# Attention with a threshold, followed by a two-layer MLP: q and k loads moved to SyncE's DMA queue, weights used two steps later

## The chip, the cores and the metric

The kernel runs on one core of a Trainium2 chip. Its engines run side by side, each with an instruction stream of its own: TensorE (PE), VectorE (DVE), ScalarE (ACT), GpSimd (POOL) and SyncE (SP), which here only issues DMAs and waits. All DMAs of the core share 16 DMA engines, whichever engine issues them. The metric is the device time of one execution in microseconds. Lower is better.

## What is computed

```python
scores = q @ k.T / sqrt(64)                       # 8 batches x 8 heads, 576 rows, 64 dims
thresh = max(scores, axis=-1) - tau               # tau = 0.02
scores = where(scores >= thresh, scores, -1e9)
attn   = softmax(scores)
x      = (attn @ v), heads side by side           # [4608, 512]
h      = x @ w_in                                 # [512, 2048]
out    = maximum(0.01 * h, h) @ w_out             # [2048, 512], result [4608, 512] fp32
```

## The kernel before

**Steps.** The attention is cut into 144 steps, 18 per batch. A step takes 128 rows of one pair of heads: its scores go to PSUM on PE (lines 333 and 339), DVE scales them and finds the row maxima (two instructions of line 393, one per head), ACT and POOL add the threshold (518, 519), DVE cuts off below it (548), and one step later ACT takes the exponential of each head (553). q and k are held as two fp16 parts (high and low), so each score is a sum of three products.

**Units and turns.** Two steps form a unit (one step in parts of the last batch). Two steps after a unit's last step, SP issues a DMA that transposes the unit's attention weights from tile w to tile wt (line 542; this is called a turn). The turn of a full unit moves 20 blocks of 128x128 fp16. A unit's last step has an odd number in its batch, so these turns are issued at odd steps. `LAG` steps after the unit's last step, PE multiplies v by the turned weights (pv, line 364), and DVE scales the result into xT, the input of the MLP (lines 374 and 380; the scale comes from wt too). From step `ENDS` = 130 on, units use `LAGE` = 4 in place of LAG. There are four wt buffers (`NWT`) and four w buffers (`NW`), two v buffers and one PSUM buffer for pv.

**The MLP.** When all four head pairs of a row block are in xT, its h units (8 matmuls each, line 248 through the helper of line 238) are put in a queue, and behind them its o units (4 matmuls each, line 265). A step takes at most one of each from the queues. ACT and DVE apply the leaky ReLU (252, 218), DVE copies a finished block of 128 output rows to osb (274), and SP stores it at the start of the next step (275). After the last step the rest of the queues is run without scores (lines 565 to 578).

**Order of the work around the change.** The order is written out by hand: the loop of line 491 puts each step's instructions in place, and two lists (`tick`, `ptick`) give what else is issued at the end of which step. The constants give the steps, counted from the start of the batch before the one that is loaded:

```python
LOADS = ((-6, 0), (2, 4))      # k and q of the first half, k and q of the second half
TURNS = ((8, 10), (14, 16))    # turns of split k and q, the same halves
VS = (-6, 0, 2, 4)             # four pieces of v, counted from the batch's own start
WOUTS = (0, 2, 4, 6, 8, 10, 12, 14)
```

`load_half` (line 95) loads k of two head pairs with one DMA (line 102) and q with two (line 105), 576 KB in each case, into tiles km and qm with two buffers each. ACT (line 156) and POOL (160, 166) split them into tiles ks and qs, and SP turns these (line 178) to kst and qst. The first batch is loaded before the loop, split by ACT and DVE, and turned by PE (line 189). v comes through POOL's queue with a cast to fp16 (line 128), as do w_in (410) and w_out (415); in the first batch these wait for an instruction of that step. So SP's queue holds, in order within a step: stores of the step before, the turn of a unit's weights, then turns of q or k. ACT's queue holds the loads of q and k between its activations.

Of the kernel before, what the change touches and what calls it, by code (L numbers as in the profile page):

```python
# [16 lines left out]
def kernel(  # L17
# [22 lines left out]
    nc = tc.nc  # L40
# [3 lines left out]
    DM = moe_w_in.shape[0]  # L44
    DF = moe_w_in.shape[1]
    C = 1.0 / (64.0 * 64.0 * 8.0)
    LAG = 5
    NARROW = 0
    NJ = DF // 128
    NEG = -1025.0  # L50
# [23 lines left out]
    if tau_f > 1.0:  # L74
# [10 lines left out]
        out=ident, in_=ident, compare_op=AX.is_equal, fill=0.0, base=0, pattern=[[-1, 128]], channel_multiplier=1)  # L85
# [9 lines left out]
    def load_half(src, store, nm, b, hb):  # L95

        m = store[b, hb] = sb.tile([128, 2, 576], FP32, tag=nm, bufs=2, name=nm)
        in_ = src[b, :, :, :].rearrange("(h f) (p t) d -> f p h (t d)", h=2, t=9)[ds(2 * hb, 2)]  # L100
        if nm == "km":
            nc.scalar.dma_start(out=m, in_=in_.rearrange("f p h x -> (f p) h x"))
        else:
            for f in range(2):
                nc.scalar.dma_start(out=m.rearrange("(p f) h x -> f p h x", f=2)[f], in_=in_[f])

    anchor = [None]

# [101 lines left out]
    def next_h():  # L210
        return hq.popleft()[0] if hq else None

    def next_o():
        return oq.popleft()[0] if oq else None
# [189 lines left out]
    for hb in range(2):  # L404
        load_half(k, kms, "km", 0, hb)
        load_half(q, qms, "qm", 0, hb)
# [50 lines left out]
    for b in range(1, B):  # L457
        s0 = 18 * (b - 1)
        for hb in range(2):
            t0 = s0 + (PREP1 if b < 2 else PREP)[hb]  # L460
            at(s0 + LOADS[hb][0], lambda b=b, hb=hb: load_half(k, kms, "km", b, hb))
            at(s0 + LOADS[hb][1], lambda b=b, hb=hb: load_half(q, qms, "qm", b, hb))
            at(t0 - 1, lambda b=b, hb=hb: hi("k", b, hb))
            at(t0 + 1, lambda b=b, hb=hb: hi("q", b, hb))

            for i, what in enumerate(("k0x", "k0l", "k1x q0x", "k1l", "q0l", "q1x", "q1l")):
                for w in what.split():
                    nm, h = w[0], int(w[1])
                    if w[2] == "x":
                        at(t0 + i, lambda nm=nm, h=h, b=b, hb=hb: after_anchor(x64(nm, b, hb, h)), ptick)  # L470
                    else:
                        for part in PARTS[nm]:
                            at(t0 + i, lambda nm=nm, h=h, b=b, hb=hb, part=part: after_anchor(lo(nm, b, hb, h, part)), ptick)
            at(s0 + TURNS[hb][0], lambda b=b, hb=hb: turn("k", b, hb))
            at(s0 + TURNS[hb][1], lambda b=b, hb=hb: turn("q", b, hb))
        for i in range(4):
            at(18 * b + VS[i], lambda b=b, i=i: load_v(b, i))
# [4 lines left out]
    for ui in range(len(units)):  # L482
        last = units[ui][3] + size[ui] - 1
        lag = LAGN if units[ui][0] < NARROW else LAG if last < ENDS else LAGE
        pv_at.setdefault(last + lag, []).append(ui)
# [4 lines left out]
    done = None  # L490
    for s in range(NS + LAG + 1):
        live = s < NS
# [6 lines left out]
        while credit >= 1.0:  # L499
            f = next_o()  # L500
            if f:
                ou.append(f)
            f = next_h()
# [8 lines left out]
        if live:  # L512
# [7 lines left out]
                out=P_[:, 0, :], in0=sa, scalar1=1.0, scalar2=bb[:, 0:1], op0=AX.mult, op1=AX.add)  # L520
            prev = (P_,) + unit_of[s]
        leak()
        for i in range(max(len(ou), len(hu))):
            o = ou[i]() if i < len(ou) else None
            h = hu[i]() if i < len(hu) else None
# [7 lines left out]
        if now is not None:  # L533
# [5 lines left out]
                out=W_[:, :, 1152:1280].rearrange("p i (h r) -> p i h r", h=2),  # L539
# [3 lines left out]
                out=uwt[now][:, 0:nw].rearrange("p i j r -> p (i j) r"), in_=W_.rearrange("p i c -> p (i c)"),  # L543
                transpose=True)
        if last is not None:
# [6 lines left out]
            for h in range(2):  # L552
                nc.scalar.activation(  # L553
                    out=uW[ui][:, i, ds(576 * h, 576)], in_=P_[:, h, :], func=AF.Exp, bias=exp_bias, scale=1.0,
# [14 lines left out]
    while hq or oq or leaky:  # L569
        for nx in (next_o, next_h):  # L570
            leak()
            f = nx()
            if f:
                f = f()
# [39 lines left out]
```

## Time and profile before

| what | value |
|---|---|
| time, median of 3 runs | 559.02 us (557.1, 559.02, 574.88) |
| the profiled execution: its time | 557.1 us |
| its span (first to last instruction) | 555.4 us |
| mean granted clock of TensorE | 0.945 |
| ACT, POOL busy | 76%, 50% of the span |
| moved by DMA | 101.79 MB, mean 183 GB/s |
| SP's DMA queue (q1), POOL's (q0), ACT's (q10) | 77.1%, 12.2%, 11.1% of 16 engines' span |
| loads of k (line 102), median issue to landing | 6.4 us, 16 of 576 KB |
| loads of q (line 105) | 5.4 us, 32 of 288 KB |
| pieces of v (line 128) | 5.4 and 6.1 us, 32 |
| turns of weights (line 542) | 6.5 us, 76 |
| stores (line 275) | 3.2 us, 36 of 256 KB |

In the views, "A <- B" means that A's engine stood idle until B was done; a DMA counts from its issue to its landing. The row of DMA digits cuts the span into 40 slices, 9 meaning 90% or more. A line of the timeline gives the start, the length, the engine (SPq and ACTq are the queues that issue DMAs), the line of the kernel and the tiles. The length of an issue on SP is the time that SP needs until it can issue the next one.

### The profile page before, as it was taken

Reading aid. Unit: us, or ns where it says so; the run is one execution under the profiler, and the core shown is the slowest. Engines: PE = TensorE matmul, PEld = TensorE weight load, DVE = VectorE, ACT = ScalarE, POOL = GpSimd, SP = SyncE. Lnnn points to the kernel's source line nnn. Section 1 sums busy time; section 2 is a strip of 40 time slices with the busy share of each in tenths; the row PEclk is TensorE's granted clock in tenths of the full one; section 3 lists DMA queues with packets and bytes.
Section 4 is the critical chain, followed back from the end, with each engine's and each line's share of the span. In section 5 each row is a group of like instructions: output and inputs, shape, how many; then the busy total and the mean of one; then the engine's idle time right before and its main releaser. Section 6 shows DMA issues by size and latency. Waiting matters only on the chain.

```text
span 555.4 us, 13438 instructions
## 1 busy us (share of the span) xinstructions
PE 473.1 (85%) x4912; PEld 294.6 (53%) x4912; DVE 464.1 (84%) x1213; ACT 424.3 (76%) x924; POOL 278.6 (50%) x476
## 2 busy tenths in 40 slices
PE   4637648898948989899888989998969999999996
PEld 3414325554625656555555655565635665666673
DVE  4936739998948999899988999999978999999641
ACT  5755728978748888888788988988886988888531
POOL 5246914668417664468446763667445764332000
PEclk9855669999979999999999999999998999999999
DMA  8999999989999899989999999989997999976611
GB/s 208 234 218 156 168 160 207 219 150 219 186 183 195 157 217 181 269 143 230 180 254 167 193 224 217 239 173 217 196 196 162 201 195 175 155 137 137 115 39 57
DMA packets 279426, 101.79 MB, mean 183 GB/s; under 512 B 254273, under 2 KB 266561, under 8 KB 279361
## 3 DMA queue, kind: packets, MB, share of 16 engines
q1 hardware_dynamic: 257344, 73.15, 77.1%
q0 software_dynamic: 13056, 8.92, 12.2%
q10 hardware_dynamic: 8960, 18.88, 11.1%
q8 instruction: 38, 0.62, 0.4%
q14 instruction: 28, 0.22, 0.1%
HBM read 36.70 MB, written 9.44 MB: 83 GB/s over the span
## 4 chain that ended last, share of the span: by engine, by line
DVE 29%; DMA 29%; issue 14%; PE 12%; POOL 11%; ACT 4%; ACTq 0%; POOLq 0%; SPq 0%; DVEq 0%
DMA wt<-w 23%; DVE sf L393 12%; DVE gT L218 5%; DVE P L548 5%; DMA v<-in_v_dram 5%; PE sc L333 4%; POOL P L519 4%; PE op L238 3%; DVE w L538 3%; PE pv L364 3%; POOL qs L166 2%; ACT w L553 2%; POOL ks L166 2%; PE hp L238 2%; DVE osb L274 2%
## 5 line engine op out<-in xcount | busy, mean ns | idle before, releaser
L393 DVE TENSOR_SCALAR_CACHE_REDUCE sf<-sc 128x576 f32<-128x576 f32 x288 | 205.4, 749 | 16.1 <-PE sc L333 15.8
L553 ACT ACTIVATE w<-P 128x576 f16<-128x576 f16 x288 | 193.8, 674 | 7.2 <-DVE P L548 2.3
L518 ACT ACTIVATE P<-sf,bb 128x576 f16<-128x576 f32 x144 | 111.3, 773 | 93.7 <-POOL bb L517 89.8
L238 PE MATMUL hp<-xT,win 128*128 128x256 f16 (+1 forms) x1344 | 151.9, 259 | 0.0
L238 PE MATMUL op<-wout,gT 128*128 128x512 f16 x576 | 148.8, 382 | 2.0 <-DVE osb L274 1.7
L333 PE MATMUL sc<-kst,qst 64*128 64x320 f16 (+1 forms) x1536 | 134.5, 301 | 11.7 <-DVE sf L393 11.2
L238 PEld LDWEIGHTS <-win 128*128 128x128 f16 x1344 | 117.7, 99 | 43.4 <-issue 2.3
L519 POOL TENSOR_SCALAR P<-sf,bb 128x576 f16<-128x576 f32 x139 | 106.0, 762 | 14.2 <-POOL bb L517 0.2
L364 PE MATMUL pv<-wt,v 128*64 128x256 f16 (+2 forms) x1000 | 59.8, 257 | 57.4 <-DMA wt<-w 52.0
L218 DVE SCALAR_TENSOR_TENSOR gT<-hp,gT 128x512 f16<-128x512 f32 x144 | 98.4, 683 | 11.3 <-ACT gT L252 11.3
L517 POOL TENSOR_SCALAR bb<-mx 128x2 f32<-128x2 f32 x139 | 27.9, 201 | 157.4 <-DVE sf L393 144.1
L333 PEld LDWEIGHTS <-qst 64*128 64x128 f16 x1536 | 73.3, 99 | 61.2 <-issue 41.2
L252 ACT ACTIVATE gT<-hp 128x512 f16<-128x512 f32 x144 | 83.5, 580 | 16.4 <-PE hp L238 16.4
L548 DVE TENSOR_SCALAR P<-P 128x1152 int16<-128x1152 int16 x144 | 81.4, 565 | 0.0
L364 PEld LDWEIGHTS <-v 128*64 128x64 f16 x1000 | 41.6, 114 | 74.5 <-issue 65.8
L238 PEld LDWEIGHTS <-gT 128*128 128x128 f16 x576 | 45.9, 98 | 64.1 <-issue 28.5
L374 DVE TENSOR_TENSOR xT<-pv,wt 128x128 f16<-128x128 f32 x128 | 32.0, 293 | 37.6 <-PE pv L364 37.5
L553 ACT ACTIVATION_READ_ACCUMULATOR w<-P 128x1 f32 x288 | 53.9, 187 | 0.0
L166 POOL TENSOR_TENSOR ks<-km,ks 128x320 f16<-128x320 f32 (+1 forms) x56 | 39.8, 731 | 9.2 <-DVE P L548 8.6
L166 POOL TENSOR_TENSOR qs<-qm,qs 128x576 f16<-128x576 f32 x28 | 35.8, 1278 | 12.4 <-DVE P L548 12.4
L538 DVE TENSOR_SCALAR w<-rc 128x256 f16<-128x256 f32 (+1 forms) x76 | 37.8, 497 | 2.6
L128 POOL DMA_DIRECT2D v<-in_v_dram x32 | 20.9, 653 | 16.9 <-DVE P L548 5.8
(35 smaller groups left out, 211.4 us busy)
## 6 DMA issues: line engine op xcount, KB each, us to landing
km<-in_k_dram ACTq DMA_DIRECT2D x16, 576.0 KB, 6.4
qm<-in_q_dram ACTq DMA_DIRECT2D x32, 288.0 KB, 5.4
out_dram<-osb SPq DMA_DIRECT2D x36, 256.0 KB, 3.2
v<-in_v_dram POOLq DMA_DIRECT2D x16, 160.0 KB, 6.1
v<-in_v_dram POOLq DMA_DIRECT2D x16, 128.0 KB, 5.4
win<-in_moe_w_in_dram POOLq DMA_DIRECT2D x8, 256.0 KB, 11.5
wout<-in_moe_w_out_dram POOLq DMA_DIRECT2D x8, 256.0 KB, 10.6
wt<-w SPq DMA_TRANSPOSE x76, 6.5
```

What stands on the lines that cost most here:

```text
L166: return nc.gpsimd.tensor_tensor(out=dst[:, h], in0=src[:, h], in1=h_[:, h], op=AX.subtract)
L218: nc.vector.scalar_tensor_tensor(out=G.g[u], in0=hp, scalar=0.01, in1=G.g[u], op0=AX.mult, op1=AX.add)
L238: nc.tensor.matmul(out=out_, lhsT=lhsT, rhs=rhs, start=start, stop=stop, skip_group_check=True)
L252: nc.scalar.activation(out=G.g[u], in_=hp, func=AF.Relu, bias=0.0, scale=0.99)
L333: nc.tensor.matmul(out=sc[h][:, cols], lhsT=qt[r, qi, ds(2 * c, 2)].rearrange("d t a b -> d (t a b)")[:, g::2], rhs=rhs, start=(i == 0), s ...
L364: nc.tensor.matmul(out=o_[ds(64 * h, 64)], lhsT=vt[:, pp, h, j, :], rhs=w_[:, :, 4 * h + j, :], start=(j == 0), stop=(j == 4), skip_group_ ...
L393: nc.vector.tensor_scalar(out=sf, in0=sc[h][:, ds(SC0, 576)], scalar1=C, scalar2=None, op0=AX.mult, op1=AX.max, accum_out=mx[:, h : h + 1])
L518: nc.scalar.activation(out=P_[:, 1, :], in_=sB, func=AF.Identity, bias=bb[:, 1:2], scale=1.0)
L519: (nc.vector if s < SPOOL else nc.gpsimd).tensor_scalar(out=P_[:, 0, :], in0=sa, scalar1=1.0, scalar2=bb[:, 0:1], op0=AX.mult, op1=AX.add)
L538: nc.vector.tensor_scalar(out=W_[:, :, 1152:1280].rearrange("p i (h r) -> p i h r", h=2), in0=rc[:, 0:nw, :].unsqueeze(3).to_broadcast([12 ...
L548: anchor[0] = nc.vector.tensor_scalar(out=pi, in0=pi, scalar1=NEG, scalar2=None, op0=AX.max)
L553: nc.scalar.activation(out=uW[ui][:, i, ds(576 * h, 576)], in_=P_[:, h, :], func=AF.Exp, bias=exp_bias, scale=1.0, accum_out=usm[ui][:, i, ...
```

## The change

LAG goes from 5 to 7, so pv of a unit stands seven steps after its last step (four from step 130 on, as before). The loads of q and k are issued by SP instead of ACT, at the same steps, behind SP's turn of the weights of the step before and behind the step's store. The first batch's loads move too. The loop runs for two steps more. The loads' sizes, the steps at which they and the turns stand, and the loads of v, w_in and w_out are the same.

```diff
-    LAG = 5
+    LAG = 7
...
         if nm == "km":
-            nc.scalar.dma_start(out=m, in_=in_.rearrange("f p h x -> (f p) h x"))
+            nc.sync.dma_start(out=m, in_=in_.rearrange("f p h x -> (f p) h x"))
         else:
             for f in range(2):
-                nc.scalar.dma_start(out=m.rearrange("(p f) h x -> f p h x", f=2)[f], in_=in_[f])
+                nc.sync.dma_start(out=m.rearrange("(p f) h x -> f p h x", f=2)[f], in_=in_[f])
```

## The prediction

> **What bounds the kernel now.** I read four views in this order. First the page's busy shares and slices:
>
> ```profile
> span 555.4 us, 13438 instructions
> ...
> PE 473.1 (85%) x4912; PEld 294.6 (53%) x4912; DVE 464.1 (84%) x1213; ACT 424.3 (76%) x924; POOL 278.6 (50%) x476
> ...
> DMA  8999999989999899989999999989997999976611
> ```
>
> No engine is full, two are close, and the DMA engines are busy in nearly every slice. Second, the waits: who stops PE and DVE?
>
> ```profile
> PE pv L364 <- DMA wt<-w: 52.0, 26, 10.0
> DVE xT L374 <- PE pv L364: 37.5, 19, 9.7
> PE pv L364 <- DMA v<-in_v_dram: 5.1, 5, 2.0
> ```
>
> (Total us, times, longest.) PE runs in program order, so when pv waits for its turned weights, everything stops. That is 57.1 us of PE standing still for two transfers; DVE idles behind it. Third, the chain of waits, start and length, where the transfer is shown from its issue to its landing, and the same place on SP's queue, on ACT's and on PE:
>
> ```profile
> 34.06 13.02 DMA wt<-w
> ...
> 61.37 15.21 DMA wt<-w
> ...
> 257.27 8.40 DMA wt<-w
> ...
> 521.06 3.63 DMA wt<-w
> ```
>
> ```profile
> 256.54 0.56 SPq L275 DMA_DIRECT2D out_dram<-osb  x1
> 257.27 10.11 SPq L542 DMA_TRANSPOSE wt<-w  x2
> 267.47 3.40 SPq L178 DMA_TRANSPOSE kst<-ks  x1
> ```
>
> ```profile
> 259.40 0.38 ACTq L102 DMA_DIRECT2D km<-in_k_dram  x1
> ...
> 265.71 0.74 PE L364 MATMUL pv<-wt,v 128*64 128x256 f16 x10 [1.82 <-DMA wt<-w]
> ```
>
> One turn of a pair's weights holds SP for about 3.0 to 3.5 us when nothing else moves, and lands some 5 us after its issue (the small ones of the end in 3.6). Beside a load of k it needs 8.4, beside w_out, k and v 13 to 15. The turn is issued two steps after its unit's last step and needed LAG - 2 = 3 steps later, so it has some 9.5 us, less the time until SP gets to it. Fourth, the stages (busy us of PE, PEld, DVE, ACT, POOL, then PE clock, DMA share, GB/s):
>
> ```profile
> 13.00:60.00 47.00, 28.43 (x219) 16.25 (x214) 32.93 (x95) 30.25 (x65) 24.65 (x39) 0.61 1.18 198
> 60.00:115.00 55.00, 40.24 (x414) 24.96 (x415) 40.16 (x105) 37.35 (x86) 27.59 (x48) 0.87 1.17 188
> ...
> 243.00:304.00 61.00, 55.01 (x574) 33.82 (x572) 56.80 (x147) 51.27 (x115) 35.36 (x61) 1.00 1.10 203
> ...
> 425.00:470.00 45.00, 44.20 (x470) 27.83 (x467) 44.42 (x120) 39.85 (x90) 27.55 (x46) 1.00 1.04 183
> ```
>
> From 425 on no q or k is loaded, pv hardly waits, and PE and DVE are both 98% busy. That is the pace without the wait. From the first L393 of each step in the timeline, batches 0 to 6 last 74.9, 59.9, 67.3, 60.6, 61.2, 59.4 and 62.7 us, and the 17 steps up to the last one 54.1. The last 10 steps of batch 6 take 31.6 us: 3.16 a step, 56.9 per batch of 18.
>
> **The change, part by part.**
> LAG 5 to 7. Every pv up to unit 64 comes two steps later. The slack of a turn grows by 2 x 3.16 = 6.3 us, from 9.5 to 15.8. The steady landings in the trace are at most 10.3 us after issue, the rare bad ones 11 to 13; pv's waits in batches 3 to 5 are 0.4 to 1.8 us each. All these fit in 6.3. What it removes at most: batches 1 to 6 sum to 371.1 against 6 x 56.9 = 341.4, excess 29.7. Batch 0 without stalls has 15 steps of about 2.97 (no h unit yet) and 3 of 3.16, 54.0, excess 20.9. Together 50.6 us. (The 57.1 us of waits are more, because DVE catches up a little after each.) The waits for v go with it: its last quarter is issued at step 18b+4 and was needed at 18b+6, now at 18b+8, 12.6 us for a transfer that takes 5.3.
>
> What LAG costs. The first h unit comes at step 15 instead of 13, and the queue serves one h and one o unit a step. Units of the last 14 steps keep their lag of 4, so the total backlog at the end grows by two pairs, run after the scores end: in the tail one pair follows the other by 1.76 us (PE op at 536.30, 538.06, 539.82). 3.5 us, less 0.4 for two early steps without an h unit: +3.1. Buffers add no wait: a wt buffer is written at last+2, read until last+7 and written again at last+10.
>
> q and k loads from SP. 16 issues of 0.40 and 32 of 0.71 us leave ACT, 29.1 us in all; ACT is 76% busy and the issues run beside its activations, so I count 0 there (if ACT were the bound, at most 3.5 us per batch). On SP they stand in order with turns and stores. In the batch from 243.3 SP issues for 48.2 us (9 turns of weights, 4 of q and k, 4 stores), then 3.5 us of loads: 51.7 of 56.9. It fits. Without room it would be 3.5 x 6 = 21 us. No load waits for a buffer in steady state: k's first half is last read at step 6 of a batch, loaded over at 12. In batch 0 the loads now wait on SP for the first pieces' readers (about 7.6, 9.8 and 13.8 us); behind them nothing is queued before the first turn at 25.7. So they run up to 9 us earlier than the 16.0 and 23.1 of now, beside v and w_in on POOL's queue, and are out of the way of the first turn. Only the fourth (step 4) comes after it.
>
> Does the shared queue slow the turns? Lower bound: no, and it helps, since a turn ahead of a load in one queue is not shared with it: down to the 5 us landing. Upper bound: each turn behind a load waits for all of it, 1.6 to 2.4 us (576 KB each; the six loads at the start land 1.77 MB in 5 us, so 1.6). Either is inside 15.8. I take 0.
>
> One page speaks against this half. The Trainium skill, "DMA: Bandwidth & Descriptors", Rules for kernel authors, says that spreading DMAs over issuing engines brings no bandwidth and saves only the issue time of the sequencer, so the ACT queue was the right place for SP's sake. By that rule alone the move is a pure cost: nothing if hidden as here, the 21 us named above if not, which would put the sum at 539 instead of 518.
>
> What stays. The DMA engines are the next limit. Counted over the packet records, fewer than 8 packets are in flight for 4.6 of the 61 us from 243 to 304, so they work 56.4 us per batch, against 56.9 for PE and DVE. That is a tie, so some waits remain: between 0 and 2 us per batch, I take 0.5, 3 us in all, since moving loads out of fine mixing with turns should shorten the work. At the start they are full (under 1 us idle from 13 to 60), so there LAG shifts the wait only once. By queue order the turn that landed at 76.6 needs everything before it: 9.5 us for the first loads, 27 for v, w_in, k, q and three pieces of w_out (9.5 to 36.5 in the trace), 5 turns of weights at 3.3, two of k and q at 3.0, three pieces of w_out at 2: 65 us, up to 70 with what mixes in. Its pv is now due at step 16, 13.8 + 16 x 2.97 + 1.6 = 63. So 2 to 7 us remain of 20.9; I take 5.
>
> Sum: 555.4 - 50.6 + 3.1 + 3 + 5 = 515.9 us span. The profiled execution took 557.1 for a span of 555.4, so 1.7 more: 517.6, say 518. Against 557.1 that is -7%; the median of the three runs shown is 559.02, 0.3% above.
>
> **The rivals.**
> A. Waits partly stay. The DMA engines get less efficient as the pace rises, and the loop settles at 59 us per batch with half of the start's stall: 555.4 - (371.1 - 354) - 10 + 3.1 + 1.7 = 533. For it: share 1.10 in steady state. Against: 4.6 us idle per batch now.
> B. The change does not do what it says: the DMA queue is the bound everywhere, later use only lengthens the queue, and LAG gains its two steps once: 555.4 - 6.3 + 3.1 + 1.7 = 554. For it: 13 to 60 is like this. Against: SP stands idle about 13 of 61 us per batch.
> C. Slower: SP's one queue becomes the bound. Place: steps 8 to 18 of each batch, where SP already issues without a gap. With loads in the same rings a turn holds SP longer, as the one at 262.26 does now (5.1 us within the 10.11 above). With 13 turns, 3.5 us of loads and 2.3 of stores per batch, the time passes 568 when the mean turn on SP passes 4.5 us (64.2 per batch); today it is 3.5 in that batch. At 4.6 a batch is 65.6 and the time 555.4 + (393.6 - 371.1) - 6.3 + 3.1 + 1.7 = 576. Against: the small stores already share this queue and the turns after them are not longer.
>
> **How the numbers follow.** Forecast 0.56, A 0.24, B 0.12, C 0.08. The forecast's own range is 503 (no residue, shorter DMA work) to 526; A covers 526 to 546. The range 503 to 546 leaves out B and C. Some 2% is what a measurement can tell from no change: 546 to 568 is "same". Faster = forecast + A = 0.80, same = B = 0.12, slower = C = 0.08.
>
> **What would show it.** PE's wait for wt falls from 52 us to under 12, most of it before 90 us; the waits for v are gone. Batches 1 to 6 last 57 to 58 us, with PE and DVE over 95% busy. SP's mean turn of weights stays under 4 us. The time from the last L393 to the end grows by 3 to 4 us. I am wrong if batches stay at 60 with pv waiting (B), or if SP never idles and turns on it take over 4.5 us (C), or if the 15.8 us is not enough because turns land over 16 us after issue.

## The result and the profile after

The changed kernel takes 536.3 us (median of 4 executions, 534.3 to 542.6), the kernel before 558.4 beside it. The ratio is 0.960 with a 95% interval of 0.955 to 0.965; on another chip it was 0.955 (0.941 to 0.968). Ratios compare only executions within 1.5% of the fastest of their kernel, while medians are of all. The profiled execution took 537.3 us for a span of 535.6. The forecast was 518 with a range of 503 to 546. The time is inside, but 18 us off, outside the forecast's own part of the range (503 to 526) and at the place of rival A (533).

The page after, the same rows as before:

```profile
span 535.6 us, 13452 instructions
...
PE 475.5 (89%) x4912; PEld 295.3 (55%) x4912; DVE 464.8 (87%) x1213; ACT 423.0 (79%) x924; POOL 279.1 (52%) x476
...
DMA  8999999999999999999999999999999999966301
```

PE and DVE do the same work as before in 20 us less, and the DMA row has lost its last digits under 9 up to the end of the scores. The waits (total us, times, longest):

```profile
PE pv L364 <- DMA wt<-w: 30.3, 19, 4.6
...
DVE xT L374 <- PE pv L364: 14.9, 7, 4.3
```

PE's wait for turned weights fell from 52.0 to 30.3, and the wait for v is gone from the list. The chain shows which turns are still late:

```profile
35.35 17.17 DMA wt<-w
...
63.34 10.68 DMA wt<-w
...
203.74 8.70 DMA wt<-w
...
265.32 6.59 DMA wt<-w
...
492.52 4.01 DMA wt<-w
```

The slack is 15.8 us now, yet turns that land 6.6 us after their issue are waited for. So their lateness arises before the issue: SP reaches them late. DVE finished the tile of the turn of 265.32 at 254.51, and SP issued without a stop in between:

```profile
253.96 0.55 DVE L538 TENSOR_SCALAR w<-rc 128x256 f16<-128x256 f32 x1
```

```profile
253.74 3.28 SPq L178 DMA_TRANSPOSE kst<-ks  x1
257.19 3.52 SPq L542 DMA_TRANSPOSE wt<-w  x1
260.80 3.68 SPq L178 DMA_TRANSPOSE qst<-qs  x1
264.58 0.57 SPq L275 DMA_DIRECT2D out_dram<-osb  x1
265.32 4.52 SPq L542 DMA_TRANSPOSE wt<-w  x1
```

Over the whole profile a turn of weights is issued 5.9 us after its tile is done (median; 10.8 at most), before the change 0.15 us (3.6 at most). In batches 1 to 6 SP's gaps between two issues that are longer than 0.3 us add up to 1.6 us, before to 67. Its queue is full: 56.5 us of issues and 2.7 us of gaps between them make the 59.2 us that a batch takes there. The stages (columns as before, the DMA share and GB/s last):

```profile
13.00:60.00 47.00, 29.14 (x222) 16.31 (x220) 32.87 (x95) 31.66 (x68) 26.48 (x42) 0.61 1.26 182
60.00:115.00 55.00, 46.71 (x494) 29.28 (x490) 49.27 (x130) 45.57 (x103) 34.34 (x58) 0.96 1.16 208
...
198.00:254.00 56.00, 54.97 (x574) 34.02 (x572) 55.19 (x148) 50.76 (x114) 35.21 (x60) 1.00 1.16 212
254.00:316.00 62.00, 57.16 (x611) 35.50 (x608) 57.48 (x148) 52.02 (x116) 36.07 (x61) 0.97 1.10 204
```

Batches 0 to 6 last 65.4, 56.5, 62.2, 56.8, 61.8, 60.9 and 56.8 us. Three of the six later ones run at the forecast pace of 56.9, the others 4 to 5 us longer, with the clock below 1. The time from the first L393 of the last step to the end grew from 42.0 to 45.8 us.

### The profile page after: what moved, and what is told of

Its sections match the earlier page's. It is cut to its first block, busy times and chain, and to the rows that moved or that the text cites. A ratio compares the mean times of both kernels' runs of the same rounds, so it can differ in the third digit from the quotient of the medians.

```text
span 535.6 us, 13452 instructions
## 1 busy us (share of the span) xinstructions
PE 475.5 (89%) x4912; PEld 295.3 (55%) x4912; DVE 464.8 (87%) x1213; ACT 423.0 (79%) x924; POOL 279.1 (52%) x476
## 4 chain that ended last, share of the span: by engine, by line
DVE 39%; DMA 20%; PE 16%; issue 13%; POOL 8%; ACT 2%; SPq 0%; POOLq 0%; DVEq 0%; ACTq 0%
DMA wt<-w 19%; DVE sf L393 16%; DVE gT L218 7%; DVE P L548 7%; PE op L238 5%; PE hp L238 4%; DVE w L538 3%; PE sc L333 3%; POOL P L519 3%; PE pv L364 3%; DVE osb L274 2%; DVE xT L374 2%; POOL ks L166 2%; DMA qm<-in_q_dram 1%; POOL bb L517 1%
## 5 line engine op out<-in xcount | busy, mean ns | idle before, releaser
L393 DVE TENSOR_SCALAR_CACHE_REDUCE sf<-sc 128x576 f32<-128x576 f32 x288 | 205.3, 749 | 15.5 <-PE sc L333 13.2
L238 PE MATMUL op<-wout,gT 128*128 128x512 f16 x576 | 150.4, 385 | 1.5 <-DVE osb L274 1.3
L333 PE MATMUL sc<-kst,qst 64*128 64x320 f16 (+1 forms) x1536 | 136.4, 300 | 15.4 <-DVE sf L393 14.2
L519 POOL TENSOR_SCALAR P<-sf,bb 128x576 f16<-128x576 f32 x139 | 107.3, 772 | 14.1
L333 PEld LDWEIGHTS <-qst 64*128 64x128 f16 x1536 | 74.7, 98 | 66.3 <-issue 45.5
L548 DVE TENSOR_SCALAR P<-P 128x1152 int16<-128x1152 int16 x144 | 84.4, 586 | 0.0
L364 PE MATMUL pv<-wt,v 128*64 128x256 f16 (+2 forms) x1000 | 56.7, 253 | 30.6 <-DMA wt<-w 30.3
L364 PEld LDWEIGHTS <-v 128*64 128x64 f16 x1000 | 39.6, 113 | 46.5 <-issue 42.4
```

Of the source, the lines that this page charges most:

```text
L238: nc.tensor.matmul(out=out_, lhsT=lhsT, rhs=rhs, start=start, stop=stop, skip_group_check=True)
L333: nc.tensor.matmul(out=sc[h][:, cols], lhsT=qt[r, qi, ds(2 * c, 2)].rearrange("d t a b -> d (t a b)")[:, g::2], rhs=rhs, start=(i == 0), s ...
L364: nc.tensor.matmul(out=o_[ds(64 * h, 64)], lhsT=vt[:, pp, h, j, :], rhs=w_[:, :, 4 * h + j, :], start=(j == 0), stop=(j == 4), skip_group_ ...
L393: nc.vector.tensor_scalar(out=sf, in0=sc[h][:, ds(SC0, 576)], scalar1=C, scalar2=None, op0=AX.mult, op1=AX.max, accum_out=mx[:, h : h + 1])
L519: (nc.vector if s < SPOOL else nc.gpsimd).tensor_scalar(out=P_[:, 0, :], in0=sa, scalar1=1.0, scalar2=bb[:, 0:1], op0=AX.mult, op1=AX.add)
L548: anchor[0] = nc.vector.tensor_scalar(out=pi, in0=pi, scalar1=NEG, scalar2=None, op0=AX.max)
```

## The experiments

Each run stands beside runs of the kernel before on the same chip, and the ratios are to those. A ring is the list of DMA packets of one issuing engine, which the 16 DMA engines work off. Theories: D, the DMA engines have no time left; S, the order of SP's one queue holds turns up; L, two steps of slack are too few. M (two rings in flight together slow each other), M3 (that takes three rings) and M2 (two suffice) came after the first runs.

**LAG alone** (two runs of one kernel): the kernel before, whose loads ACT issues, with

```diff
-    LAG = 5
+    LAG = 7
```

> LAG 7, the loads of q and k left on ACT's queue: the first half of the change alone. Three theories of why the change gave 21 us and not 40. D: the 16 DMA engines are the limit (57 to 58 us of work per batch against 56.9 for PE and DVE), so which queue issues hardly matters: 530 to 545, within 1.5% of the changed kernel's 536. S: SP's single queue is the limit, since loads now stand ahead of turns: without them the batches run at 56.9 and the time is 520 or less. L: two steps of slack are still too few: as D for this run.

> LAG 7 with the loads on ACT's queue once more, beside the next run on one chip. In its first profile the DMA engines did the same work as in the others (414 us, each packet at the lower quartile of its kind) but were busy for 503 us instead of 470 to 476: 30 us went in jams such as the one from 157 to 177, where packets of SP's, ACT's and POOL's rings are in flight together. The 14 extra loads on ACT cost no more than those on SP, so M in its plain form is out. M3: jams need three rings, and the loads of q and k stand at the steps of the loads of v. All: 545 to 590 with a wide scatter.

Eight executions: 554.3, 571.5, 582.1, 588.7 in the first run, 539.6, 556.1, 561.0, 563.8 in the second, against medians of 554.1 and 558.6 for the kernel before. They scatter too much for an interval: the fastest of each run are at 1.00 and 0.97 of the kernel before, the other six between 556 and 589. The half of the change that was to give everything gives no gain that this scatter lets one see. D's 530 to 545 is missed as well as S's 520: without loads on SP's queue no execution comes near it. But something else slows this kernel, which could hide a gain, so S is settled only by the run without v below. The profile of the 571 us execution shows what (stages, columns as above):

```profile
157.00:177.00 20.00, 6.39 (x88) 4.31 (x88) 7.39 (x20) 8.68 (x20) 7.76 (x12) 0.76 1.23 128
182.00:200.00 18.00, 17.79 (x177) 10.90 (x174) 17.40 (x44) 16.51 (x38) 12.38 (x21) 1.00 1.08 189
```

```profile
150.89 24.75 DMA wt<-w
```

For 20 us the DMA engines are full (share 1.23) and move 128 GB/s, and one turn lands 24.75 us after its issue; 5 us later they move 189 GB/s at a lower share. In this jam packets of SP's ring, of ACT's and of POOL's are in flight together, and a packet of a turn takes 59 ns in the mean where its median is 18. I summed over all packets of an execution what each would take at the lower quartile of its kind, over 16 engines, and compared it with the time in which at least 8 packets are in flight:

| kernel | work, us | busy, us |
|---|---|---|
| before | 414 | 473 |
| after; again | 414; 415 | 474; 470 |
| LAG alone; again | 414; 414 | 503; 487 |
| queue alone | 415 | 476 |
| LAG 9 | 415 | 484 |

With LAG 7 and the loads on ACT's ring the same work takes 13 to 33 us more DMA time than in the changed kernel. The two profiles are of executions some 17 us above the fastest of their runs, and LAG 9 with one ring takes 10 to 14 more too, so the totals alone don't blame the second ring. The jams do: cut into stretches of 8 us from 132 us on, the worst stretch loses 3.2 to 4.9 us against that work in the kernels of this document in which ACT issues loads (the kernel before among them), and 2.0 to 2.7 in the others, LAG 9 among them (the profile of 1536 us below is left out).

**The queue alone:** `LAG = 5`, loads on SP.

> LAG 5, the loads of q and k on SP's queue: the second half alone. D: no less DMA work, so 550 to 560, as before the change; at best 545, as the fine mixing of loads and turns (three bad spots of 4 to 7 us in the trace of before) goes. S: slower than before, 565 or more, since turns wait behind loads and have 9.5 us instead of 15.8. L: between 550 and 565.

546.1 us, ratio 0.988 (0.981 to 0.996). As D expected at its better end, and not slower, against S. So the queue alone gives 1.2%, LAG alone nothing that can be told from its scatter, and both together 4 to 4.5%.

**More slack:**

```diff
-    LAG = 7
+    LAG = 9
-    NWT = 4
+    NWT = 5
```

> LAG 9 with five wt buffers in place of four, loads on SP. L: another 6.3 us of slack takes the rest of pv's waits: 11 us of the start and most of 14 us in batches 1 to 6 go, less 3.5 us for two more pairs of MLP units at the end: 515 to 518. D: the slack moves the backlog once, by at most 6.3 us, and the tail takes 3.5 to 4 back: 531 to 537, with waits of pv still there in batches 2 to 6. S: as D.

546.4 us, ratio 0.983 (0.975 to 0.991): slower than LAG 7. L falls, and D was missed too, in the number and in its sign: pv does not wait in batches 1 to 6 at all. The waits, and one batch's place of it:

```profile
PE sc L333 <- DMA qst<-qs: 22.4, 7, 5.4
...
PE pv L364 <- DMA wt<-w: 16.1, 6, 7.0
```

```profile
207.00:212.00 5.00, 2.20 (x20) 1.17 (x14) 3.97 (x12) 4.97 (x13) 2.42 (x5) 1.00 1.00 164
212.00:214.00 2.00, 0.00 (x0) 0.00 (x0) 0.00 (x0) 0.71 (x3) 0.00 (x0) 0.94 1.23 293
214.00:218.00 4.00, 3.89 (x23) 1.98 (x24) 2.23 (x6) 0.48 (x1) 0.60 (x2) 0.60 1.06 194
```

The turns of weights now have time, and the next thing behind on SP's queue is late in their place: the turn of q, on which the scores wait 3 to 5 us in five of these six batches. A turn of weights is now issued 8.2 us after its tile is done (median). A long stop also costs more than its length: after the one shown PE's clock is 0.60 from 214 to 218. At the start ACT waits 11 us for w buffers whose turn has not been made, since there are still four of them.

**Half the added slack:** `LAG = 6`, loads on SP.

> The changed kernel with LAG 6: slack 12.6 us in place of 15.8, one pair of MLP units less behind the last scores (1.8 us). D: slack moves the backlog and adds no DMA time, so it lies between LAG 5 and LAG 7: about 3 us more of waits in batch 0, more of the turns that land 10 to 11 us after issue waited for: a ratio of 0.965 to 0.98 to the kernel before, 539 to 547. If it is as fast as LAG 7 or faster, most of the seventh step is not needed.

538.0 us, ratio 0.965 (0.954 to 0.976): at the edge of what D expected, and not to be told from LAG 7. By lag 5, 6, 7, 9 the ratios are 0.988, 0.965, 0.955 to 0.960, 0.983.

**Less DMA work.** First the changed kernel again, on the chip of the next three:

> The changed kernel itself, beside the next three on one chip. LAG alone gave no gain (554 to 589 in four runs) and the queue alone 1.2%, so theory S is out, and a new one stands: M, loads of q and k on ACT's ring and turns on SP's ring, in flight together, slow each other down; LAG 7 keeps both rings full, so it needs the single ring. D stands beside it: the DMA engines are the limit of what is left. All theories: 530 to 540.

531.9 us (526.2 to 536.6). Then the loads of v, which are on POOL's queue, left out from batch 2 on, so later batches use the v of batches 0 and 1:

```diff
         if i == 0:
             vts[b] = vbufs[b % 2]
+        if b >= 2:
+            return
```

> The changed kernel without the loads of v from batch 2 on, so batches 2 to 7 multiply with the v of batches 0 and 1. SP's queue is as it was; some 4.4 us of DMA work per batch (counted by packet lengths) go from POOL's queue. D: batches 2 to 6 sum to 303 in the profile after and fall to 285 to 288 (56.9 each), waits of pv there nearly gone: 518 to 523. M: v's ring mixes with SP's too, so the same sign; but if only ACT's ring mattered, 530 or more. S: 532 or more.

520.5 us, ratio 0.940 (0.927 to 0.952). Batches 2 to 6 take 56.7, 56.2, 56.6, 56.2 and 56.5 us (282.2, against 292.6 for the changed kernel beside it; 298.5 in the profile after, where the expectation said 303). One of them:

```profile
247.50:304.00 56.50, 56.06 (x610) 35.44 (x609) 56.19 (x148) 51.43 (x115) 33.04 (x56) 1.00 1.11 211
```

PE and DVE are busy over 99% of it, and every wait for turned weights in batches 2 to 6 goes. SP's queue holds the same instructions in the same order and is as full as in the changed kernel, but in batches 1 to 6 a turn holds it for 3.60 us in the mean, against 3.86. So S as it was put is out: some 4.1 us less DMA work per batch (packets at their lower quartile), on another ring, shorten SP's turns and with them its queue. D holds in this form: the DMA engines are the limit, and PE feels it through SP's full queue. That POOL's ring no longer mixes with SP's would have the same sign; this run does not tell it from the amount, the next one does. Whether fewer issues on SP, at the same DMA work, would do as much is not tested. This is the pace that the forecast gave to the change.

**More DMA work:** a load of 576 KB into an unused tile at steps 6 and 14 of each batch, once from SP, once from ACT.

```diff
+    for b in range(1, B):
+        for s_ in (6, 14):
+            ...
+            at(18 * (b - 1) + s_, lambda in_x=in_x: nc.sync.dma_start(out=extra, in_=in_x...))
```

> The changed kernel with two more loads of 576 KB per batch (14 in all), into a tile that nobody reads, issued by SP at steps 6 and 14. D: each is 1.6 to 1.8 us of DMA work, and nothing is left to hide it: 14 x 1.7 = 24 us more, 555 to 563; a little less if the 2 to 3 us per batch of idle DMA time take some. M: the same, since it is one ring. If the DMA engines were not the limit: under 545.

> The same 14 extra loads, at the same steps, issued by ACT. D alone: as on SP, 553 to 563. M: two rings in flight again, 6 to 10 us per load in the jams: 575 to 620 and a wide scatter between runs.

From SP 570.8 us, ratio 1.020 (1.000 to 1.039); from ACT 564.4, ratio 0.991 (0.982 to 1.001), which rests on two of ten executions. D's sign is right and its size too small: by the ratios some 36 us more than the changed kernel for 14 loads on SP, 2.6 each (39 us by the medians), where packet lengths say 1.5. On SP no other ring was added, so the amount counts by itself: in batches 1 to 6 a turn holds SP for 4.12 us there. M as first put falls: 14 loads on a second ring at these steps cost no more than on SP.

**Two rings, not three:** the loads on ACT, LAG 7, and no v from batch 2 on (so v of batches 0 and 1 is used).

> LAG 7, q and k loads on ACT, and no loads of v from batch 2 on (batches 2 to 7 use the v of batches 0 and 1), so from there on only two rings carry data. M3: the jams of batches 2 to 6 go and the time comes to that of the same kernel with SP's loads, 520, at most 530. M2 (two rings suffice for jams): the loss of some 30 us stays, 540 or more.

529.7 us, ratio 0.946 (0.938 to 0.954), beside 0.940 with the loads on SP. The time is just inside M3's bound of 530 and 9 us above the kernel with the loads on SP; the profile decides:

```profile
152.00:160.00 8.00, 4.42 (x77) 3.03 (x76) 5.30 (x14) 6.30 (x14) 4.69 (x9) 1.00 1.24 146
160.00:168.00 8.00, 4.51 (x36) 2.71 (x37) 5.84 (x14) 5.94 (x14) 3.82 (x6) 0.94 1.31 97
200.00:240.00 40.00, 40.00 (x408) 24.57 (x408) 39.52 (x106) 37.22 (x82) 23.23 (x42) 1.00 1.08 218
```

Here v is not loaded any more, and still the engines sink to 97 GB/s at a share of 1.31. So M3 falls: SP's and ACT's rings suffice for a jam. But it is the last one. From batch 3 on the batches run at 56.4 with the loads on ACT just as well, and in batches 4 to 6 SP stands idle for 6 to 8 us each: there its queue is not full. That a jam needs turns queued up on SP when ACT's loads arrive is a guess from its place. What else it takes is open: with the 14 extra loads from ACT, SP's turns were late throughout (5.7 us in the median), and only one stretch lost as much (from 412 to 428).

**The start:** w_in at steps 1 to 15, w_out four steps later.

```diff
-    WOUTS = (0, 2, 4, 6, 8, 10, 12, 14)
+    WOUTS = (4, 6, 8, 10, 12, 14, 16, 18)
+    WINS = (1, 3, 5, 7, 9, 11, 13, 15)
```

> The changed kernel, with the eight pieces of w_in loaded at steps 1 to 15 instead of all at the start, and w_out four steps later (steps 4 to 18). The 11 us of waits in batch 0 of the profile after come either from order (w_in and w_out ahead of the first turns): then batch 0 falls from 65 to 56 us and the time by 8 to 10, to 524 to 528; or from the amount, which is only put off (some 100 us of DMA work up to step 24 against 87 us of steps): then batch 0 gains 5, batch 1 loses as much, and the time stays at 530 to 537. I expect the second.

545.0 us, ratio 0.966 (0.955 to 0.978): no gain over the changed kernel, and outside both of the expected ranges. In its profile batch 0 takes 75.2 us, 10 more than in the profiles of the changed kernel, where the expectation had it gain 5, and by the packet count the DMA engines now stand idle for 7.7 us between 13 and 60, where they were full: the loads come later, where there is no room. So this run does not show whether order or amount makes the waits of the start; that stays open.

With LAG 8 on top:

> As the run before, with LAG 8: half of the added slack of LAG 9, where turns of q and no longer turns of weights came late (4 to 5 us of waits for qst in each batch). D: within 1.5% of the run before, since slack adds no DMA time; a new wait for qst of 1 to 3 us per batch would show that the backlog only moves.

553.3 us, ratio 0.989 (0.981 to 0.997), 2.3% behind the run before and not within the expected 1.5%. The profiled execution took 1536 us, so it does not show whether a wait for qst came up.

## Why the prediction held, and where it did not

*What bounds the kernel.* Right that pv's wait for turned weights is what stops PE, and that 56.9 us a batch is the pace without it: 56.2 to 56.7 when DMA work is taken out. The wait fell to 30.3 us, not under 12 as the forecast's sign had it; 12.4 of that are in batch 0, 15.7 in batches 1 to 6.

*LAG removes up to 50.6 us.* The change removed 25.6: batches 1 to 6 take 355.0 us, not 341.4 to 344, and batch 0 65.4, not 59. The reasoning that landings of at most 10.3 us fit in 15.8 counted from the issue on SP. At the new pace SP comes to a turn 5.9 us late in the median and up to 10.8, and the slack is eaten ahead of the issue.

*The step that failed* is the sum for SP's queue, "51.7 of 56.9. It fits", and with it the term for what stays, "between 0 and 2 us per batch, I take 0.5", which measured 2.3 (13.6 in six). SP's issues took 56.5 us per batch, with 2.7 us of gaps between them that the sum left out. Of the 4.8 us over 51.7, turns that hold SP longer make 4.3: 13 of them at 3.86 us in the mean, where the batch that was summed has 3.53. The tie of the DMA engines was read rightly: at least 8 packets are in flight for 56.5 us per batch before, and for 57.1 and 56.6 in the two profiles of the changed kernel, whose batches last 59.2 and 58.1.

*The start and the end.* At the start 11.4 us remained where I took 5 (range 2 to 7); there the DMA engines are full. The end cost 1.9 us in the last 17 steps and 3.8 after them, 5.7 in all, where the sum had 3.1 for it. The sum's own reading of the end before was off too: the 17 steps take 53.6 us there, not 54.1.

*A size that the sum did not have at all:* a stop of about 2 us can cost 3.4, as below. Batches 2, 4 and 5 take 5.4, 5.0 and 4.1 us more than batch 3. Longer waits of pv (5.3, 4.5 and 3.6 us, against 0.8) are most of it; each of the three, and no other of batches 1 to 6, also has one stretch of 3.4 us at half the clock.

*The queue half counted at 0* was wrong, though its direction was named ("it helps, since a turn ahead of a load in one queue is not shared with it"). Without it LAG 7 shows no gain beyond its scatter. The rule of the Trainium skill ("DMA: Bandwidth & Descriptors", Rules for kernel authors) that spreading over issuing engines buys no bandwidth agrees with these runs. The pure cost that it would make of the move did not come about: at LAG 7 the kernel took 577 and 559 us in the median with the loads on the second ring, 536 and 532 with them on SP's.

*Rivals.* A gave the numbers: 59.2 us a batch (it said 59), half of the start left. Its reason, that the DMA engines get less efficient as the pace rises, shows for 0.1 to 0.6 us of DMA time a batch only, so its number was in part luck. B falls for the whole kernel. C falls by its number, since the mean turn on SP took 3.8 us (weights 4.07, where I had said under 4), below 4.5, and the time fell; but its place and half of its sign came true: in the later batches SP never idles. The range held because it took in A.

## What to carry to other kernels

When a wait is removed, ask what the resource behind it can give at the new pace, and take the tie as a loss. Sum an issuing queue with the gaps between its issues and with issues as long as they are beside full DMA engines: here 51.7 us became 59.2. More slack for one user of a full queue only makes the next user late. Before giving two issuing engines a ring each for the sake of their sequencers, look whether transposes and loads are in flight together and at what GB/s.

## What the runs showed that I had not expected

After a stop of only about 2 us PE's granted clock can fall to half, for some 3.4 us. In the changed kernel, around a wait of 2.06 us that ends at 339.85:

```profile
336.00:340.00 4.00, 1.94 (x23) 1.24 (x22) 3.18 (x8) 4.00 (x10) 2.97 (x5) 1.00 1.12 242
340.00:342.00 2.00, 2.00 (x53) 1.23 (x49) 0.67 (x2) 0.82 (x4) 0.68 (x2) 0.78 1.27 248
342.00:344.00 2.00, 2.00 (x8) 0.88 (x7) 1.97 (x7) 0.47 (x1) 0.59 (x2) 0.50 0.97 241
344.00:346.00 2.00, 2.00 (x20) 1.17 (x19) 1.00 (x3) 1.29 (x3) 1.41 (x2) 0.86 0.94 310
```

Four matmuls of line 238 take 1.89 us there and 1.04 us elsewhere. The step lasts 5.49 us and the next 4.08, against 3.15 and 3.0 at the same place of batch 3: 3.4 us lost for 2.06 of waiting. A wait of 1.94 us that ends at 271.95 was followed by the same (0.50 from 274 to 276). In the kernel before, a wait of 1.82 us that ends at 265.71 left the clock at 1.00, and so did one of 1.97 at 178.65:

```profile
178.00:182.00 4.00, 3.35 (x33) 2.07 (x35) 2.35 (x7) 2.03 (x7) 1.76 (x5) 1.00 0.67 140
...
264.00:268.00 4.00, 2.29 (x26) 1.38 (x26) 2.87 (x6) 2.95 (x8) 1.86 (x4) 1.00 1.32 150
```

The Trainium skill ("TensorE: Matmul & The Clock Gate", Part 1) states that the clock is halved after an idle window of about 3.4 us. Here 1.94 and 2.06 us were enough, so the measurement stands; since 1.97 us was not enough elsewhere, the length of the stop alone does not decide it.
